# A range check on the softmax sums, a guarded second program behind a branch, and an instruction order read from a list

## The chip, the cores and the metric

The kernel runs on one core of a Trainium2 chip. A core has five instruction streams that run side by side and meet at semaphores: PE (TensorE, the matrix engine), ACT (ScalarE), DVE (VectorE), POOL (GpSimd) and SP (SyncE, which here only issues DMA transfers). The metric is the device time of one execution in microseconds. A change of under 0.2% of this kernel's time is treated as no change.

## The reference

The program is one transformer block for 2048 tokens of width 1024: an adaptive layer norm, attention with 32 query heads that share one key and one value head of width 32, and a gated feed-forward network of width 3584. Six modulation vectors come from a conditioning vector. Cut to what matters:

```python
mod = (_silu(c) @ w_mod).reshape(c.shape[0], 6, 1, -1)
sa, ca, ga, sb, cb, gb = ...
h = _layernorm(x, axis=-1) * (1 + ca) + sa
q, k, v = h @ wq, h @ wk, h @ wv            # 32 heads of 32; one k, one v
scores = jnp.einsum('bhqd,bkd->bhqk', q, k) * Dh ** (-0.5)
p = softmax(scores, axis=-1)                # the maximum of each query is subtracted
o = jnp.einsum('bhqk,bkd->bhqd', p, v)
x = x + ga * (o @ wo)
h = _layernorm(x, axis=-1) * (1 + cb) + sb
x = x + gb * ((_silu(h @ w1) * (h @ w3)) @ w2)
```

## The kernel before

The 2048 tokens are cut into 8 blocks of 256 queries (`n`), and the 32 heads into 8 groups of 4 (`f`). One pair (n, f) is a unit, so there are 64 units. A unit goes through the 2048 keys in 8 steps of 256 keys. One such step, `s_exp` (line 950), is called a score block here: 8 matmuls fill four PSUM banks with scores (tile `S<-QT,KT` in the profile), and ACT takes the exponential of them in two instructions of 128x1024 (`U<-S`). There are 512 score blocks, numbered S0 to S511 in this text in the order of PE's stream, and 1024 exponentials. The scores are not shifted: exp is taken of the scaled score as it is, and the division by the sum comes at the end.

What follows a score block: `pairs` and `fold` (lines 970, 979) add the exponentials on DVE (`PS<-U`, `PS<-PS`); `dens` (line 993) finishes the sums on PE with a matrix of ones (`PB<-PS,ONES`); `av_mm` (line 984) multiplies by the values (`PB<-U,V`, 64 matmuls for a unit); `attend` (line 1024) takes the reciprocal of the sums on DVE (`RC<-RB`), spreads it and scales the result into `QT`.

When the 8 units of a block of queries are done, its output projection (`wo`), its second layer norm, 14 pieces of the gated network (`slab`: 64 matmuls on `W`, one tanh on ACT, two products on DVE) and 4 pieces of the last matrix (`quarter`: 56 matmuls on `W2S`) follow. PE does them in between the score blocks of the next block of queries. So ACT has the exponentials all the time, and PE has, after each score block, some filling work from the block before. After S511 the last block's network is left for PE alone.

Many of the filling matmuls exist in two forms: one product of 128x128 weights, or four products of 32-row column tiles beside each other (`32x256` and `32x512` rows); the form is picked when the order is made.

The order of the work is made when the kernel is built. `build` describes each piece of work as a node of a graph with an engine (or two to choose from), a duration, a due time `vt` and the keys it reads and writes. `Placer.run` (line 294) then places the nodes one by one: `choose` (line 365) takes, for each engine, the candidate with the smallest due time among those that could start soon, and the engine that could start first gets its piece. The table `PLAN` (line 116) holds, for every 8 score blocks, the tolerances of that choice and offsets to the due times by kind of work and engine. `commit` gives a session of PE work one of the free PSUM banks (two of the eight, `PB`, until the last exponentials free the others). `emit` works out the semaphore waits. The result is one fixed list of instructions for each engine; all of them are played through `play` at line 22, so every instruction of the profile has the line L22, and the tiles tell them apart.

At the end SP waits for the transfers of the output (`finish`, L527) and all engines leave the block (L531).

The lines that the change touches, beside the table:

```python
            best = None
            for e, lst in ready.items():
                c = self.choose(e, lst)
...
    pl.run()
    pl.finish("sp", outs)
    pl.emit_all()
```

Of the kernel before, what the change touches and what calls it, by code (L numbers as in the profile page):

```python
# [8 lines left out]
P = 128  # L9
# [33 lines left out]
class Graph:  # L43
# [64 lines left out]
    def alias(self, new, old):  # L108
# [7 lines left out]
PLAN = [  # L116
    (0, 0.08, 0.11, 0, 1.1, {"an/dve": 11, "av/dve": 9, "d0/sp": -38, "d1/sp": 10, "d11/sp": 2, "d12/sp": -4,
     "d2/sp": 51, "d3/sp": -151, "d6/sp": 67, "d7/sp": 32, "d8/sp": -29, "ev/act": -21, "k/pe": -26, "k/dve": 40,
     "ln/pe": -51, "ln/act": 32, "ln/dve": -11, "ln/pool": 57, "mc/pe": 52, "mc/sp": -2, "mod/pe": -62,
     "mod/dve": 10, "nm/act": 79, "pair/dve": -129, "q/pe": 3, "q/dve": -57, "quarter/pe": 11, "quarter/dve": -2,  # L120
     "s/pe": 67, "s/act": -3, "slab/pe": -5, "slab/act": 81, "slab/dve": 30, "v/pe": -8, "wo/pe": -78, "wo/dve": 1,
     "wo/sp": 36}),
    (0, 0.36, 0.11, 1, 1, {"an/dve": 8, "av/pe": -111, "av/dve": 2, "d0/sp": -31, "d1/sp": 16, "d10/sp": -66,
     "d12/sp": 63, "d13/sp": -1, "d3/sp": -14, "d5/sp": 2, "d7/sp": 84, "d8/sp": -2, "ev/act": -29, "k/pe": -36,
     "k/dve": -9, "kb/pe": 72, "ln/dve": 124, "mod/dve": -5, "nm/act": 32, "pair/dve": -104, "quarter/dve": 2,
     "s/pe": 55, "s/act": 107, "slab/pe": -26, "slab/act": -5, "slab/dve": 33, "slab/sp": 94, "v/dve": -118,
     "v/pool": -34, "wo/pe": -76, "wo/dve": 4, "wo/pool": -59, "wo/sp": 21, "d11/sp": 0, "d2/sp": 0, "d6/sp": 0,
     "ln/pe": 0, "ln/act": 0, "ln/pool": 0, "mc/pe": 0, "mc/sp": 0, "mod/pe": 0, "q/pe": 0, "q/dve": 0,
     "quarter/pe": 0, "v/pe": 0}),
    (0, 0.14, 0.18, 2, 2.9, {"q/dve": -32, "wo/dve": -44, "slab/act": 0}),  # L130
    (0.06, 0.11, 0.27, 0, 3.9, {"av/dve": 9, "d0/sp": -58, "d1/sp": 20, "d10/sp": 257, "d13/sp": 2, "d2/sp": 3,
     "d3/sp": -2, "d4/sp": 1, "d8/sp": 83, "ev/act": -11, "k/pe": -49, "k/dve": 1, "kb/dve": -7, "ln/pe": -5,
     "mc/pe": 63, "mc/sp": 5, "nm/act": 30, "out/sp": 1, "s/act": 114, "slab/sp": 4, "v/dve": 3, "v/pool": -26,
     "wo/pe": -78, "wo/dve": 14, "wo/pool": -23, "an/dve": 0, "d12/sp": 0, "d7/sp": 0, "ln/dve": 0, "mod/dve": 0,
     "pair/dve": 0, "q/dve": 0, "quarter/dve": 0, "s/pe": 0, "slab/pe": 0, "slab/dve": 0, "wo/sp": 0, "av/pe": 0,
     "d5/sp": 0, "kb/pe": 0}),
    (0, 0.11, 0.05, 0, 0.6, {"d6/sp": 19, "ev/act": -9, "k/pe": -81, "wo/pool": 7, "s/act": 0}),
    (0, 0.11, 0.05, 0, 0.6, {}),
    (0.13, 0.12, 0.23, 0, 0.7, {"av/pe": -5, "d0/sp": -4, "d10/sp": -68, "d3/sp": -46, "d9/sp": 72, "ev/act": -16,
     "kb/pe": 2, "ln/dve": -11, "mc/pe": -7, "mod/dve": -3, "q/dve": -85, "q/sp": -6, "quarter/pe": 4,  # L140
     "slab/act": 82, "slab/dve": 33, "slab/sp": 16, "wo/pe": -5, "wo/dve": 3, "wo/pool": 15, "av/dve": 0,
     "d1/sp": 0, "d2/sp": 0, "d6/sp": 0, "k/pe": 0, "k/dve": 0, "ln/pe": 0, "mc/sp": 0, "nm/act": 0, "d13/sp": 0,
     "v/dve": 0, "v/pool": 0, "d4/sp": 0, "kb/dve": 0, "out/sp": 0}),
    (0.24, 0.09, 0.2, 1, 1.4, {"av/pe": -4, "d7/sp": 78, "ev/act": -13, "ln/pool": -2, "mod/pe": 5,
     "pair/dve": -16, "slab/act": 83, "d0/sp": 0, "mod/dve": 0}),
    (0.24, 0.09, 0.02, 1, 0.4, {"d2/sp": -4}),
    (0.07, 0.17, 0.24, 1, 0.1, {"d1/sp": 31, "d3/sp": 24, "d6/sp": 8, "d7/sp": -38, "ev/act": 20, "k/dve": 31,
     "kb/pe": 6, "ln/dve": -16, "ln/pool": 60, "mc/pe": 2, "mc/dve": 35, "nm/act": -28, "out/sp": 2,
     "pair/dve": -28, "q/dve": -49, "quarter/pe": -1, "slab/act": 10, "v/dve": 20, "wo/pool": -13, "d2/sp": 0,
     "d8/sp": 0, "mod/pe": 0, "slab/dve": 0, "wo/pe": 0, "wo/dve": 0, "d10/sp": 0, "slab/sp": 0, "d9/sp": 0,  # L150
     "q/sp": 0}),
    (0, 0.11, 0.17, 2, 2.8, {"d7/sp": -42, "k/dve": 34, "mod/dve": -56, "slab/act": -17, "q/dve": 0, "out/sp": 0}),
    (0, 0.11, 0.2, 2, 2.8, {"ev/act": 21}),
    (0, 0.11, 0.24, 1, 3.2, {"d1/sp": 8, "d3/sp": 21, "d7/sp": -38, "ev/act": 20, "k/dve": 31, "mod/dve": -60,
     "pair/dve": -30, "slab/act": 10, "v/pe": 39}),
    (0, 0.11, 0.24, 1, 3.2, {}),
    (0, 0.16, 0.15, 1, 3.2, {"d1/sp": 31, "d3/sp": 24, "kb/pe": 10, "ln/dve": -15, "mc/dve": 38, "q/dve": -16,
     "v/dve": 2, "v/pe": 0}),
    (0.06, 0.11, 0.15, 1, 0.1, {"d1/sp": 7, "ln/pool": 59, "pair/dve": -45, "v/dve": 24, "q/dve": 0}),
# [97 lines left out]
class Placer:  # L257
# [6 lines left out]
    FULL = 36.0  # L264
    FETCH = 24.0

    def __init__(self, g, banks, later, plan):
        self.g = g
        self.plan = []
        off = {}  # L270
# [1096 lines left out]
```

## Time and profile before

| what | value |
|---|---|
| time, median of 3 runs | 1136.85 us (1136.72, 1136.85 and 1138.08) |
| the profiled execution, first to last instruction | 1137.5 us; the page lists no other time of it |
| PE busy | 1102.1 us, 97% |
| DVE busy | 989.8 us, 87% |
| ACT busy | 1020.1 us, 90% |
| POOL busy | 39.1 us, 3% |
| mean granted TensorE clock | 0.992 |
| transfers | 209.64 MB, mean 184 GB/s |

The page names the instructions by tile (out<-in), since they share one line. "Idle before" and the bracket in a row of the timeline give how long the engine stood still ahead of that instruction and what it then got; "issue" there means that it waited for nothing that the profile shows. PEld is the weight load of PE, which runs beside its matmuls.

### The profile page before, as it was taken

Reading aid. Unit: us, or ns where it says so; the run is one execution under the profiler, and the core shown is the slowest. Engines: PE = TensorE matmul, PEld = TensorE weight load, DVE = VectorE, ACT = ScalarE, POOL = GpSimd, SP = SyncE. Lnnn points to the kernel's source line nnn. Section 1 sums busy time; section 2 is a strip of 40 time slices with the busy share of each in tenths; the row PEclk is TensorE's granted clock in tenths of the full one; section 3 lists DMA queues with packets and bytes.
Section 4 is the critical chain, followed back from the end, with each engine's and each line's share of the span. In section 5 each row is a group of like instructions: output and inputs, shape, how many; then the busy total and the mean of one; then the engine's idle time right before and its main releaser. Section 6 shows DMA issues by size and latency. Waiting matters only on the chain.

```text
span 1137.5 us, 37371 instructions
## 1 busy us (share of the span) xinstructions
PE 1102.1 (97%) x16835; PEld 752.4 (66%) x16860; DVE 989.8 (87%) x1617; ACT 1020.1 (90%) x1159; POOL 39.1 (3%) x91
## 2 busy tenths in 40 slices
PE   5999998999899999999999999999999999999998
PEld 4744536766467766777577766776567757776887
DVE  7998999999989989998999899998989899997442
ACT  5999999999999999999999999999989999994110
POOL 5200000000000000000000000000000000000000
PEclk9999989999999999999999999999999999999999
DMA  9320586675756666865596577868686558767993
GB/s 347 104 76 22 166 217 187 193 205 139 168 150 194 190 176 160 240 190 151 137 287 192 151 190 202 227 193 216 142 245 192 156 152 226 210 198 197 239 240 103
DMA packets 381535, 209.64 MB, mean 184 GB/s; under 512 B 17600, under 2 KB 373184, under 8 KB 381376
## 3 DMA queue, kind: packets, MB, share of 16 engines
q1 hardware_dynamic: 380944, 207.11, 65.9%
q8 instruction: 133, 2.18, 0.8%
q14 instruction: 26, 0.21, 0.1%
q10 hardware_dynamic: 432, 0.13, 0.0%
HBM read 199.89 MB, written 4.19 MB: 179 GB/s over the span
## 4 chain that ended last, share of the span: by engine, by line
PE 48%; ACT 42%; DVE 6%; DMA 1%; issue 1%; SPq 1%; POOL 0%; DVEq 0%
ACT U L22 39%; PE PB L22 34%; PE S L22 14%; ACT HT L22 3%; DVE PS L22 2%; DMA W<-in_A_wq_dram 1%; DVE ST L22 1%; SPq L22 1%; DVE X L22 1%; DVE RB L22 0%; DVE QT L22 0%; DVE HT L22 0%; DVE XNB L22 0%; DVE WO L22 0%; DVE MV L22 0%
## 5 line engine op out<-in xcount | busy, mean ns | idle before, releaser
L22 ACT ACTIVATE U<-S 128x1024 bf16<-128x1024 f32 x1024 | 966.6, 1142 | 11.5 <-PE S L22 10.7
L22 DVE TENSOR_TENSOR PS<-U 128x2048 bf16<-128x2048 bf16 x256 | 308.2, 1216 | 12.0 <-ACT U L22 10.1
L22 DVE TENSOR_TENSOR PS<-PS 128x1024 bf16<-128x1024 bf16 (+1 forms) x420 | 282.5, 689 | 2.5
L22 PE MATMUL PB<-QT,W 128*128 128x256 bf16 (+1 forms) x2688 | 228.1, 276 | 0.4 <-DVE HT L22 0.4
L22 PE MATMUL S<-QT,KT 32*128 32x256 bf16 x4096 | 204.7, 274 | 10.1 <-ACT U L22 7.8
L22 PEld LDWEIGHTS PB<-QT,W 128*128 128x128 bf16 (+1 forms) x2688 | 171.2, 98 | 42.0 <-issue 23.6
L22 PE MATMUL PB<-W2S,HT 128*128 128x256 bf16 x1512 | 189.3, 273 | 0.0
L22 PEld LDWEIGHTS PB<-W2S,HT 128*128 128x128 bf16 x1512 | 137.4, 98 | 41.5 <-issue 22.0
L22 PEld LDWEIGHTS S<-QT,KT 32*128 32x128 bf16 x4096 | 60.8, 92 | 139.5 <-ACT U L22 130.9
L22 PE MATMUL PB<-U,V 128*32 128x256 bf16 x4096 | 130.9, 276 | 3.5 <-issue 2.3
L22 PEld LDWEIGHTS PB<-U,V 128*32 128x32 bf16 x4096 | 101.8, 97 | 27.8 <-issue 15.3
L22 PE MATMUL PB<-QT,HT 128*128 128x256 bf16 (+1 forms) x1216 | 117.0, 273 | 0.0
L22 PE MATMUL PB<-HT,W 128*32 128x512 bf16 (+2 forms) x884 | 99.2, 343 | 3.1 <-DVE XNB L22 1.0
L22 PEld LDWEIGHTS PB<-QT,HT 128*128 128x128 bf16 (+1 forms) x1216 | 86.4, 97 | 21.0 <-issue 11.4
L22 ACT ACTIVATE HT<-PB 128x512 bf16<-128x512 f32 (+1 forms) x105 | 77.0, 733 | 7.9 <-PE PB L22 7.8
L22 DVE SCALAR_TENSOR_TENSOR HT<-HT,PB 128x512 bf16<-128x512 bf16 x100 | 68.3, 683 | 6.7 <-ACT HT L22 6.5
L22 PEld LDWEIGHTS PB<-HT,W 128*128 128x128 bf16 (+1 forms) x896 | 50.6, 97 | 34.3 <-issue 13.4
L22 DVE TENSOR_TENSOR HT<-HT,PB 128x512 bf16<-128x512 bf16 x100 | 68.2, 682 | 4.4 <-PE PB L22 3.1
L22 ACT ACTIVATE HT<-S 128x512 bf16<-128x512 f32 (+1 forms) x17 | 12.1, 721 | 58.9 <-PE S L22 58.9
L22 DVE STREAM_TRANSPOSE RB<-PB 128x256 f32<-128x256 f32 x63 | 28.0, 444 | 33.8 <-PE PB L22 33.4
L22 PE MATMUL PB<-WO,QT 128*128 128x512 bf16 (+1 forms) x260 | 53.2, 381 | 1.4 <-issue 0.6
L22 POOL TENSOR_SCALAR RS<-MV 128x1 f32<-128x1 f32 x32 | 10.2, 322 | 1009.3 <-DVE MV L22 1008.6
(111 smaller groups left out, 661.7 us busy)
## 6 DMA issues: line engine op xcount, KB each, us to landing
W<-in_B_w_dram SPq DMA_DIRECT2D x150, 512.0 KB, 4.6
W2S<-in_B_w_dram SPq DMA_DIRECT2D x30, 1792.0 KB, 8.5
HT<-in_B_w_dram SPq DMA_DIRECT2D x74, 512.0 KB, 4.7
W2S<-in_w_mod_dram SPq DMA_DIRECT2D x8, 1024.0 KB, 6.3
X<-in_A_x_dram SPq DMA_DIRECT2D x8, 512.0 KB, 7.2
U<-in_w_mod_dram SPq DMA_DIRECT2D x4, 1024.0 KB, 12.2
out_dram<-X SPq DMA_DIRECT2D x7, 512.0 KB, 7.7
W2S<-in_A_x_dram SPq DMA_DIRECT2D x5, 512.0 KB, 9.7
```

The costliest lines, as they stand in the source:

```text
L22: return getattr(e, call[0])(*call[1], **call[2])
```

## The change

Four things change.

1. The reciprocals of the sums are kept for a whole block of queries (`RC` grows from 8 to 2x8x8 columns), and after the 8 units of a block two small DVE instructions on 128x64 (`in_range`) multiply into a tile `FINE` whether each reciprocal lies between 1e-18 and 1e18. `FINE` is set to 1 by POOL at the start. That is 16 instructions.
2. `verdict`: after the last block one DVE reduction, one PE matmul of 1 column with the ones matrix and one DVE comparison write the tile `AGAIN`, which is 1 if any reciprocal was out of range.
3. At the end of its list every engine waits for `AGAIN`, loads it into a register, and branches: if it is not 0, a second, complete program runs, in which `shift` finds each query's maximum and three more matmuls for each head subtract it ahead of the exponential. It stands in each engine's instruction stream behind the branch. SP's wait for the output transfers, which stood behind its last transfer, now stands behind the branch.
4. The table `PLAN` is replaced for the first program by `ORDER`, a list of all 7306 nodes in the order in which they are to be placed, with a mark (`b`) where the second engine is to be taken. `choose` is still called, with the one node of the list as its candidate. The second program is still placed by the rule, with one row of `PLAN`.

The diff, cut to its core (the body of `build` is moved one level in, as `program(guarded)`, which the cut leaves out):

```diff
-PLAN = [
-    (0, 0.08, 0.11, 0, 1.1, {"an/dve": 11, "av/dve": 9, "d0/sp": -38, "d1/sp": 10, "d11/sp": 2, "d12/sp": -4,
...
+PLAN = [(0, 0.11, 0.15, 1, 2.0, {})]
+
+
+ORDER = """
+7 1 11 0 4 2 5 8 3 6 16 12 9 13 10 17 18 60 22 15 19 59 20 27 14 21 28 412 29 37 30 31 23 24 26 32 36 77 33 38 61 39
...
-            for e, lst in ready.items():
+            lists = ready
+            if self.order:
+                i, k = self.order[len(g.nodes) - left]
+                assert g.nodes[i].npred == 0
+                lists = {g.nodes[i].alts[k][0]: [g.nodes[i]]}
+            for e, lst in lists.items():
                 c = self.choose(e, lst)
...
+        def both(eng, name):
+            for fn in self.ops[name]:
+                fn(eng)
+            eng.wait_ge(sem[flag.sem], flag.val)
+            again = eng.value_load(tile)
+            with eng.If(again != 0):
+                for s, v in last.items():
+                    if v:
+                        eng.wait_ge(sem[s], v)
+                for fn in second.ops[name]:
+                    fn(eng)
+            if name == "sp":
+                for n in outs:
+                    eng.wait_ge(sem[n.sem], n.val)
...
+    LOW, HIGH = 1e-18, 1e18
...
-    RC = sb("RC", [P, 8], F32)
+    RC = sb("RC", [P, 2, NC, 8], F32)
+    FINE = sb("FINE", [P, NC, 8], BF16)
+    FINE1 = sb("FINE1", [P, 1], BF16)
+    AGAIN = sb("AGAIN", [P, 1], mybir.dt.int32)
...
+        if not guarded:
+            op("pool", lambda: [lambda e: e.memset(FINE[:], 1.0)], 0.1, writes=["FINE"], vt=-100)
...
+                    if guarded:
+                        calls += [lambda e, g=g, t=t, kk=kk: e.matmul(
+                            BANK[2 * r[g // 2] + g % 2][:, kk * B:(kk + 1) * B], ONES[:], SHIFT[:, t, g, :], start=False,
+                            stop=t == 2) for t in range(3) for g in range(4)]
...
+            rc = RC[:, n % 2, f]
+            op("dve", lambda: [lambda e: e.reciprocal(rc, RB[:, 0, :].rearrange("p (a r) -> p a r", r=32)[:, :, 0])],
+               0.12, reads=["RBD"], writes=[("RC", n % 2, f)], vt=vt)
...
+        def in_range(n):
+            G.tag = "ok"
+            k = [("RC", n % 2, f) for f in range(NC)]
+            for lim, cmp in ((LOW, ALU.is_ge), (HIGH, ALU.is_le)):
+                op("dve", lambda lim=lim, cmp=cmp: [lambda e: e.scalar_tensor_tensor(
+                    FINE[:], RC[:, n % 2], lim, FINE[:], cmp, ALU.mult)], 0.15, reads=k + ["FINE"], writes=["FINE"], vt=64.0 * n + 80)
+
+        def verdict():
+            G.tag = "ok"
+            vt = 64.0 * NB + 20
+            op("dve", lambda: [lambda e: e.tensor_reduce(FINE1[:], FINE[:].rearrange("p a b -> p (a b)"), mybir.AxisListType.X,
+                                                         ALU.min)], 0.15, reads=["FINE"], writes=["FINE1"], vt=vt)
+            s = Sess()
+            op("pe", lambda b: [lambda e: e.matmul(BANK[b][:, 0:1], ONES[:], FINE1[:], start=True, stop=True)], 0.07,
+               reads=["ONES", "FINE1"], writes=["sum"], vt=vt, mode="F", sess=s, post=0.145)
+            return op("dve", lambda b: [lambda e: e.tensor_scalar(AGAIN[:], BANK[b][:, 0:1], P - 0.5, None, ALU.is_lt)], 0.1,
+                      reads=["sum"], writes=["AGAIN"], vt=vt, sess=s)
...
+    pl, outs, flag = program()
+    second, outs2, _ = program(True, pl)
+    second.finish("sp", outs2)
+    pl.emit_all(second, flag, AGAIN[0:1, 0:1], outs)
```

How far the list departs from the order before: on PE 3694 of the 4112 common pieces of work stand in the same relative order, on DVE 1150 of 1608, on ACT 1135 of 1155, on SP 277 of 309. Counted at every 32nd score block, PE has had the same amount of filling work by then in both orders, and behind S511 the same 433 pieces are left to it, with the verdict's matmul as one more. So the list moves work by a few places.

The first place is PE from S79 to S82, where the first block of queries has gone over to its network. `PB<-U,V` is a unit's product with the values, `PB<-HT` and `PB<-HT,W` are the network's products, `PB<-PS,ONES` finishes the sums. Before:

```order
L22 MATMUL PB<-HT,W 128x256 x12
L22 MATMUL S<-QT,KT 128x256 x8
L22 MATMUL PB<-HT,W 128x256 x14
L22 MATMUL S<-QT,KT 128x256 x8
L22 MATMUL PB<-PS,ONES 32x256 x4
L22 MATMUL PB<-U,V 32x256 x64
L22 MATMUL PB<-HT 32x256 x8
L22 MATMUL S<-QT,KT 128x256 x8
L22 MATMUL PB<-HT 32x256 x48
L22 MATMUL S<-QT,KT 128x256 x8
L22 MATMUL PB<-HT 32x256 x8
L22 MATMUL PB<-HT 128x256 x10
```

After:

```order
L22 MATMUL PB<-HT,W 128x256 x20
L22 MATMUL S<-QT,KT 128x256 x8
L22 MATMUL PB<-HT,W 128x256 x6
L22 MATMUL PB<-PS,ONES 32x256 x4
L22 MATMUL S<-QT,KT 128x256 x8
L22 MATMUL PB<-HT 128x256 x12
L22 MATMUL S<-QT,KT 128x256 x8
L22 MATMUL PB<-U,V 32x256 x64
L22 MATMUL PB<-HT 128x256 x4
L22 MATMUL S<-QT,KT 128x256 x8
L22 MATMUL PB<-HT 128x256 x14
```

The run of 64 value products, which stood right behind the sums and ahead of 8 column-tile matmuls, now stands ahead of S82 instead of S81, while the sums have gone from ahead of S81 to ahead of S80, and the network's products there have all become 128-wide.

The second place is PE around S375, some six blocks of queries in. Before:

```order
L22 MATMUL PB<-QT,HT 128x256 x8
L22 MATMUL PB<-QT,W 128x256 x8
L22 MATMUL S<-QT,KT 128x256 x8
L22 MATMUL PB<-PS,ONES 32x256 x4
L22 MATMUL PB<-QT,W 32x256 x96
L22 MATMUL S<-QT,KT 128x256 x8
L22 MATMUL PB<-W2S,HT 128x256 x12
```

After:

```order
L22 MATMUL PB<-QT,HT 128x256 x10
L22 MATMUL PB<-QT,W 128x256 x8
L22 MATMUL S<-QT,KT 128x256 x8
L22 MATMUL PB<-PS,ONES 32x256 x4
L22 MATMUL PB<-QT,W 32x256 x64
L22 MATMUL S<-QT,KT 128x256 x8
L22 MATMUL PB<-QT,W 128x256 x8
L22 MATMUL PB<-W2S,HT 128x256 x4
```

The unbroken run of 4 and 96 column-tile matmuls is cut to 4 and 64; the rest comes after the next score block, in the 128-wide form.

The third place is PE around S409 to S411. Before:

```order
L22 MATMUL PB<-PS,ONES 32x256 x4
L22 MATMUL PB<-QT,W 32x256 x32
L22 MATMUL S<-QT,KT 128x256 x8
L22 MATMUL PB<-U,V 32x256 x64
L22 MATMUL PB<-QT,W 32x256 x8
L22 MATMUL S<-QT,KT 128x256 x8
L22 MATMUL PB<-QT,W 32x256 x48
L22 MATMUL S<-QT,KT 128x256 x8
L22 MATMUL PB<-QT,W 32x256 x8
```

After:

```order
L22 MATMUL PB<-PS,ONES 32x256 x4
L22 MATMUL PB<-QT,W 32x256 x40
L22 MATMUL S<-QT,KT 128x256 x8
L22 MATMUL PB<-QT,W 32x256 x56
L22 MATMUL PB<-U,V 32x256 x8
L22 MATMUL S<-QT,KT 128x256 x8
L22 MATMUL PB<-U,V 32x256 x24
L22 MATMUL PB<-QT,W 32x256 x24
L22 MATMUL PB<-U,V 32x256 x8
L22 MATMUL S<-QT,KT 128x256 x8
L22 MATMUL PB<-U,V 32x256 x24
L22 MATMUL PB<-QT,W 32x256 x8
```

The value products of the unit, which were one run of 64, are spread over three gaps and mixed with the network's column-tile matmuls.

The fourth is the end of DVE's stream. Before:

```order
L22 TENSOR_TENSOR HT<-S,GBR 128x256
L22 TENSOR_TENSOR X<-X,HT 128x256
L22 TENSOR_TENSOR HT<-S,GBR 128x256
L22 TENSOR_TENSOR X<-X,HT 128x256
L531 UNCONDITIONAL_BRANCH
```

After:

```order
L22 TENSOR_TENSOR HT<-PB,GBR 128x256
L22 TENSOR_TENSOR X<-X,HT 128x256
L22 TENSOR_TENSOR HT<-S,GBR 128x256
L22 TENSOR_TENSOR X<-X,HT 128x256
L719 TENSOR_LOAD AGAIN
L720 COMPARE_AND_BRANCH
```

DVE's last work is unchanged; what was the jump out of the block is now the load of `AGAIN` and the branch past the second program. The same pair has been put at the end of each of the other four streams.

More of the change, by code (lines that the diff above doesn't have):

```diff
@@ L265, with __init__ @@
     FETCH = 24.0
-    def __init__(self, g, banks, later, plan):
+    def __init__(self, g, banks, later, plan, first=None, order=None):
         self.g = g
@@ L292, in __init__, with read @@
         self.warm = None
+        self.order = self.read(order) if order else None
+        if first is not None:
+            self.sem, self.dma_sem = first.sem, first.dma_sem
+            self.count, self.dma_cnt = dict(first.count), dict(first.dma_cnt)
+            for e in self.ops:
+                self.known[e] = first.finals()
+    @staticmethod
+    def read(order):
+        seq = []
+        for x in order.split():
+            k = int(x[-1] == "b")
+            a, _, z = x.rstrip("b").partition("-")
+            seq += [(i, k) for i in range(int(a), int(z or a) + 1)]
+        return seq
     def run(self):
```

1617 lines of the change are left out of this document (889 added, 728 removed), and 45 rows, old and new, of tables (ORDER, PLAN).

## The prediction

> **What bounds the kernel now.** I read the page first (busy shares, chain), then the stages, then ACT's own waits.
>
> ```profile
> span 1137.5 us, 37371 instructions
> PE 1102.1 (97%) x16835; PEld 752.4 (66%) x16860; DVE 989.8 (87%) x1617; ACT 1020.1 (90%) x1159; POOL 39.1 (3%) x91
> PE 48%; ACT 42%; DVE 6%; DMA 1%; issue 1%; SPq 1%; POOL 0%; DVEq 0%
> ```
>
> PE and ACT share the chain, so the stages have to be told apart:
>
> ```profile
> core 0: us, PE busy (x) PEld busy (x) DVE busy (x) ACT busy (x) POOL busy (x), PEclk, DMA share, GB/s
> 440.00:680.00 240.00, 239.10 (x3684) 165.31 (x3681) 221.35 (x351) 238.83 (x274) 1.95 (x4) 1.00 0.72 197
> 1040.00:1137.50 97.50, 94.64 (x867) 81.24 (x860) 39.33 (x72) 8.36 (x14) 1.69 (x4) 1.00 0.78 206
> ACT U L22 <- PE S L22: 10.7, 15, 2.2
> ```
>
> In the middle ACT works 238.83 of 240 us on exponentials and the tanh, so it sets the pace, and PE is just in time for it: over the whole run ACT stands ahead of an exponential for only 10.7 us, 15 times. DVE has 18.65 us free of 240. In the last 97.5 us the exponentials are over and PE alone is the bound (94.64 busy; the rest is the end, where the last DVE work and the last transfer follow). So an order of PE's work can win at most those 10.7 us ahead of the last exponential, and nothing behind it, since the same 433 pieces remain there. Whatever is put behind the last transfer or beside it can only lengthen the end.
>
> **The moved work, place by place.** ACT's larger waits by place:
>
> ```profile
> 149.09 7.51 ACT L22 ACTIVATE U<-S 128x1024 bf16<-128x1024 f32 x8 [0.67 <-PE S L22]
> 157.33 14.83 ACT L22 ACTIVATE U<-S 128x1024 bf16<-128x1024 f32 x16 [0.73 <-PE S L22]
> 172.67 6.59 ACT L22 ACTIVATE U<-S 128x1024 bf16<-128x1024 f32 x7 [0.51 <-PE S L22]
> 187.40 1.93 PE L22 MATMUL PB<-U,V 128*32 128x256 bf16 x64 [0.59 <-DVE HT L22]
> 189.94 2.86 ACT L22 ACTIVATE U<-S 128x1024 bf16<-128x1024 f32 x3 [1.19 <-PE S L22]
> 391.81 48.80 ACT L22 ACTIVATE U<-S 128x1024 bf16<-128x1024 f32 x53 [0.47 <-PE S L22]
> 763.77 2.79 PE L22 MATMUL PB<-QT,W 128*32 128x256 bf16 x96
> 766.94 3.77 ACT L22 ACTIVATE U<-S 128x1024 bf16<-128x1024 f32 x4 [0.47 <-PE S L22]
> 834.55 0.29 PE L22 MATMUL PB<-U,V 128*32 128x256 bf16 x4 [2.33 <-issue]
> 835.46 1.94 ACT L22 ACTIVATE U<-S 128x1024 bf16<-128x1024 f32 x2 [2.18 <-PE S L22]
> 838.49 1.94 ACT L22 ACTIVATE U<-S 128x1024 bf16<-128x1024 f32 x2 [1.09 <-PE S L22]
> 840.59 1.02 ACT L22 ACTIVATE U<-S 128x1024 bf16<-128x1024 f32 x1 [0.16 <-PE S L22]
> ```
>
> S375 (766.94): a run of 96 matmuls took 2.79 us and ACT then waited 0.47. In the list a third of the run goes to the next gap; two thirds take 1.9, which is 0.9 shorter than the run that cost 0.47. Term: -0.47; at worst 0. The same run stands unchanged at other block edges (391.81 is one), so their 0.47 stays.
>
> S81 (189.94): PE waited 0.59 for DVE, which had yet to free the bank, did 64 value products in 1.93 and 8 more matmuls; ACT waited 1.19. In the list these products come one score block later, ahead of S82, when DVE is through, and with 4 network matmuls behind them: a gap below the 2.79 that costs 0.47, with no wait in front. Ends: -1.19 if nothing is left, 0 if the wait moves along to S82. I take -0.9, near the first, because the longest run in the trace leaves under half as much.
>
> S61 to S73 (149 to 173): three waits, 1.91 together. The modulation chunk's matmuls go one gap earlier and one output-projection piece is evened out. DVE is what PE waits for there, and its amount of work stays. Ends: -1.9 and +1; I take -0.3, nearest to no change.
>
> S410 (834.55): PE stopped for 2.33 us inside one run of 64 matmuls, waiting for nothing that the profile shows, and ACT lost 2.18 + 1.09 + 0.16 = 3.43. What surrounds it:
>
> ```profile
> DMA  9999999999999999999999999999999999999999
> q8 instruction: 1, 0.02, 0.9%
> q8 instruction: 133, 2.18, 0.8%
> ```
>
> The first two lines are for 828 to 836 us: every slice has the transfer engines full, and one 16 KB packet of instructions came in. The third is the whole run: 133 such packets, one in 8.6 us on average (1137.5/133). Around S410 column-tile matmuls of 29 ns each (2.79/96), with a weight load each, eat instructions faster than elsewhere. So I read the stop as instructions that came late; that is an inference. The list mixes the 64 value products with other column tiles (156 of them in the three gaps up to S411 become 164), which keeps that stretch as dense. I take it as staying: 0. If it goes, -3.43; that is the first rival.
>
> Head: the scaled first columns of `wq` go from six on DVE and two on POOL to five and three.
>
> ```profile
> 24.28 2.03 POOL L22 TENSOR_SCALAR WO<-W,MODC 128x256 bf16<-128x256 bf16 x2 [1.68 <-DMA W<-in_A_wq_dram]
> 27.11 0.14 DVE L22 COPY QBI<-PB 128x2 f32<-128x2 f32 x1
> 27.30 0.77 PEld L22 LDWEIGHTS PB<-HT,WO 128*128 128x128 bf16 x8 [0.97 <-DVE QBI L22]
> ```
>
> PE started the first query projection at 27.30, on DVE's copy. Three tiles on POOL end at 24.28 + 3 x 1.02 = 27.34, so +0.1 at most. SP's early transfers are only exchanged among themselves ahead of the same one of `wq`. ACT has two evacuations instead of two norms after the first exponential, about as long. Term: 0.
>
> **The added work.**
>
> ```profile
> L22 DVE RECIPROCAL RC<-RB 128x8 f32<-128x8 f32 x64 | 12.9, 201 | 1.8
> L22 DVE COPY VBR<-PB 128x32 f32<-128x32 f32 x1 | 0.2, 182 | 0.0
> L22 DVE TENSOR_TENSOR V<-PB,VBR 128x128 bf16<-128x128 f32 x4 | 1.2, 288 | 0.1
> 160.00:170.00 10.00, 9.84 (x91) 3.77 (x92) 9.83 (x17) 10.00 (x12) 0.79 (x2) 1.00 1.14 287
> ```
>
> A check on 128x64 lies between 182 and 288 ns; I take 0.22. Sixteen of them, the reduction and the comparison make 18 x 0.22 = 4.0 us of DVE. In a block of 125 us there are 2 of them, 0.44, against some 9.7 us free (18.65 x 125/240): hidden. In the first block they come after S67, between the waits at 157 and 173, where DVE is full (9.83 of 10 in the last row); there up to 0.44 reaches ACT. Term: +0.2 (0 to +0.44). What waits behind them is an evacuation or a pair sum. The verdict's matmul lies in the last stage, where PE is the bound: one column, behind a reduction that comes right after the last `QT`; other products stand between. Term +0.1 (0 to 0.5). The comparison is long done when the flag is read. POOL's memset runs while POOL waits for the first data: 0.
>
> **The end.** All engines now load `AGAIN` and branch. PE and ACT do so while DVE still works; DVE and SP are last.
>
> ```profile
> 1125.21 10.64 SPq L22 DMA_DIRECT2D out_dram<-X  x4
> 1135.19 0.29 DVE L22 TENSOR_TENSOR X<-X,HT 128x256 bf16<-128x256 bf16 x1
> SPq L527 <- DMA out_dram<-X: 0.9, 1, 0.9
> SPq L531 <- PEq L531: 0.2, 1, 0.2
> SCC<-in_c_dram ACTq DMA_DIRECT2D x1, 2.0 KB, 2.4
> 0.72 0.10 POOL L22 MEMSET NH<- 128x1 f32 x1 [0.29 <-POOLq L1352]
> ```
>
> SP issued its last transfer by 1135.85 and then waited 0.9 for it. Load and branch go into this 0.9, and what is longer is added. The trace has no register load: below it is bounded by a message between sequencers (0.2), above by the smallest transfer from issue to landing (2.4). I take 0.9, a third of the way, since it is one word and needs no descriptors. The branch jumps over a whole program: below, the start's barrier and jump took 0.29; above, 2.33, the stop at 834.55 if that was a late instruction packet. I take 1.6, nearer to the upper, since the target lies behind some hundred transfers on SP and thousands of instructions on DVE. Sum 0.9 + 1.6 - 0.9 = +1.6; from 0 (0.2 + 0.29 is hidden) to 2.4 + 2.33 - 0.9 = +3.8.
>
> The Trainium skill speaks against this change here: "Runtime: NRT & Kernel Launch", Instruction fetch mechanics, says that a taken branch whose target is outside the two-page window must wait until that page is fetched, and "DMA: Bandwidth & Descriptors", Latency and other measured facts, gives a register load some 0.6 us at least. Before's trace has no such branch to confirm it. With 0.6 for the load and 2.33 for the fetch the end would be an estimated +2.0.
>
> **Sum.** -0.47 - 0.9 - 0.3 + 0.2 + 0.1 + 1.6 = +0.2. Against the profiled execution's 1137.5 that is 1137.7; the median of the three runs, 1136.85, stands 0.65 lower, so I forecast 1137.1. A difference of 0.2%, 2.3 us, is about what a measurement of this kernel can tell from no change.
>
> **Rivals.**
>
> Faster: the stop at S410 does not come back, because packets and transfers meet differently. For it: it came once in 512 gaps, and the list takes apart the very run in which it came. Against it: the stretch stays as dense and the transfers as full. Time: 1137.1 - 3.4 = 1133.7.
>
> Slower by the end: load and jump at their upper ends, +3.8 instead of +1.6: 1139.3. For it: two things on SP one after the other with only 0.9 of cover. Against it: the transfer queues are idle then. It decides from an end of 3.7 on (2.3 + 1.4 of the other terms).
>
> Slower by the order: the list makes new long gaps ahead of S79, S82, S238 and S383 (20 products, or 64 column tiles and 4 products). If each costs 0.47 as the 2.79 run does, S81 and S61 to S73 win nothing and the checks cost 0.44: 1136.85 - 0.47 + 1.9 + 0.44 + 0.1 + 1.6 = 1140.4. Against it: the order before has such gaps too, and ACT waits only 15 times in all.
>
> The change does not do what it says: a reciprocal counts as out of range and the second program runs, at least 1137 more, some 2300 us. Against it: sums over 2048 keys of small scores are far from 1e18.
>
> **Chances.** Forecast 0.45 (own range 1135.3 to 1139.0: S81 and S61 to S73 at their gains, or the end near 3.5), stop gone 0.25, end at its upper bound 0.15, order with new waits 0.13, second program 0.02. Faster by over 0.2% (below 1134.6): most of the stop's case, 0.20, and 0.04 of the forecast's: 0.24. Slower (above 1139.1): 0.11 of the end's case, 0.11 of the order's, 0.02, and 0.06 of the forecast's: 0.30. Within 0.2%: 0.46. The range reaches from the stop's case to the order's: 1133.3 to 1140.4.
>
> **What would show it.** The changed profile should have no wait of ACT at S375 and under 0.5 at S81 to S82; 0.47 still at the other block edges; a stop of PE on "issue" near S410 of about 2 us; DVE checks of about 0.22 us; the last DVE work as long before the end as now plus 1.6, with SP on a load and a jump. I am wrong if ACT's waits ahead of exponentials sum to over 14 us or under 6, or if the end after DVE's last work grows by over 3.

## The result, and the profile after

The changed kernel takes 1139.8 us (median of 20 runs, 1137.88 to 1141.51); the kernel before, in 20 runs beside it, 1137.71. The ratio is 1.0018, 95% interval 1.0012 to 1.0025: some 2.1 us slower, a bit under the 0.2% bound, which lies inside the interval. The second program did not run.

The page of the changed kernel, the lines that answer to those of before (the first is the span, the second busy time by engine, the third the chain that ended last, the others the queues that bring instructions):

```profile
span 1138.1 us, 37341 instructions
PE 1102.5 (97%) x16818; PEld 753.6 (66%) x16845; DVE 993.6 (87%) x1634; ACT 1020.1 (90%) x1159; POOL 42.8 (4%) x93
PE 47%; ACT 44%; DVE 3%; DMA 2%; issue 1%; SPq 1%; POOL 1%; DVEq 0%
q8 instruction: 134, 2.20, 0.8%
q14 instruction: 33, 0.27, 0.1%
```

Bounds and chain are as before. One thing has to be read rightly first: a span is not the time of the execution. In every run here, of all the kernels, the time lies 1.7 to 2.1 us above the span (the changed kernel's profiled execution took 1140.01 us at a span of 1138.1; the kernel before has 1137.9 at 1136.0 in one run, 1135.55 at 1133.6 in another). So the profile of before that the prediction was made from, span 1137.5, belongs to an execution of some 1139.4 us, 1.7 above that kernel's median: it shows one of its slow executions.

**ACT's waits** by place, of the changed kernel, and their sum over the run (last line: total, times, longest):

```profile
152.87 3.77 ACT L22 ACTIVATE U<-S 128x1024 bf16<-128x1024 f32 x4 [0.96 <-PE S L22]
157.94 12.98 ACT L22 ACTIVATE U<-S 128x1024 bf16<-128x1024 f32 x14 [1.31 <-PE S L22]
171.49 7.58 ACT L22 ACTIVATE U<-S 128x1024 bf16<-128x1024 f32 x8 [0.56 <-PE S L22]
391.51 54.42 ACT L22 ACTIVATE U<-S 128x1024 bf16<-128x1024 f32 x59 [0.50 <-PE S L22]
782.11 38.99 ACT L22 ACTIVATE U<-S 128x1024 bf16<-128x1024 f32 x42 [0.55 <-PE S L22]
835.65 2.86 ACT L22 ACTIVATE U<-S 128x1024 bf16<-128x1024 f32 x3 [0.25 <-PE S L22]
961.26 2.85 ACT L22 ACTIVATE U<-S 128x1024 bf16<-128x1024 f32 x3 [0.42 <-PE S L22]
ACT U L22 <- PE S L22: 7.5, 14, 1.3
```

The waits at S81 (1.19 before) and S375 (0.47 at 766.94) are gone, and of the 3.43 at S410 0.25 is left. In their place stand 0.55 at 782.11 (S383), 0.42 at 961.26 (S476), and 2.83 instead of 1.91 between 149 and 173. Three PE rows belong to this:

```profile
151.25 1.01 PE L22 MATMUL PB<-SCC,W2S 128*128 128x1 bf16 x32 [1.65 <-DMA W2S<-in_w_mod_dram]
834.75 0.29 PE L22 MATMUL PB<-QT,W 128*32 128x256 bf16 x4 [0.34 <-issue]
1069.67 0.39 PE L22 MATMUL S<-QT,W 128*128 128x256 bf16 x2 [0.75 <-DVE HT L22]
```

The modulation chunk's matmuls, one gap earlier in the list, wait 1.65 us for their own weights; the 2.33 us stop is down to 0.34; and the last stage has a new wait for DVE.

**The end.** First the last DVE work of the changed kernel, then, in the order of time, the flag's loads on DVE and SP, their branches, and what each does next (L730 and L728); the last line is the kernel before, SP's waits behind its last transfer. Columns of the lower rows: count, shortest/median/longest in ns, first and last start:

```profile
1133.43 0.29 DVE L22 TENSOR_TENSOR X<-X,HT 128x256 bf16<-128x256 bf16 x1
```

```profile
L719 DVEq TENSOR_LOAD <-AGAIN x1: 545/545/545, 1133.5 to 1133.5; - x1
L719 SPq TENSOR_LOAD <-AGAIN x1: 502/502/502, 1134.2 to 1134.2; - x1
```

```profile
L720 DVEq COMPARE_BRANCH  x1: 72/72/72, 1134.0 to 1134.0; - x1
L720 SPq COMPARE_BRANCH  x1: 53/53/53, 1134.7 to 1134.7; - x1
```

```profile
L730 DVEq DRAIN  x1: 57/57/57, 1137.0 to 1137.0; - x1
```

```profile
L728 SPq EVENT_SEMAPHORE  x6: 17/28/28, 1137.3 to 1137.7; - x6
```

```profile
L527 SPq EVENT_SEMAPHORE  x6: 17/28/28, 1135.9 to 1137.1; - x6
```

The load is 0.50 us; the branch itself is short, but then nothing happens on SP for 2.58 us (1134.75 to 1137.33) and on DVE for 2.9. In that hole the trace has this, from 1134.9 to 1136.2, where the program's own transfers move next to nothing:

```profile
q8 instruction: 1, 0.02, 6.3%
q14 instruction: 2, 0.02, 3.9%
```

By the transfer records the two packets of 8 KB on q14 land at 1135.52 and 1135.98. The records do not name the engine that a packet is for. If the first is DVE's, which branched first, and the second SP's, DVE goes on (1136.99) 1.47 us behind its own, and SP (1137.33) 1.35. From DVE's last work to the end it is 4.41 us, against 2.06 before: +2.35.

**Where the time went**, by ACT's 1024 exponentials. Each column is the lateness that a stretch added against the profile of before (negative: it won). The e2 column is the old order with everything else of the change, the next four have the list; e1, e3 and e4 are told below:

| stretch of exponentials | e2 (old order) | changed kernel | e1 | e3 | e4 |
|---|---|---|---|---|---|
| up to the first exponential | +0.14 | +0.30 | +0.26 | +0.33 | +0.56 |
| 0 to 116 | 0.00 | -0.45 | -0.49 | -0.45 | +0.58 |
| 116 to 154 (S58 to S77) | +0.14 | +1.18 | +0.02 | +2.09 | +0.58 |
| 154 to 158 (S79) | +0.01 | +0.29 | +0.29 | +0.29 | +0.28 |
| 158 to 170 (S81) | -0.01 | -0.87 | -0.86 | -0.87 | -0.87 |
| 170 to 304 (S139, S145, S151) | +0.09 | -0.92 | -0.92 | -0.88 | -0.91 |
| 304 to 748 (S274 to S280 above all) | +0.05 | +0.70 | +0.65 | +0.65 | +0.65 |
| 748 to 768 (S375, S383) | 0.00 | +0.16 | +0.16 | +0.16 | +0.16 |
| 768 to 816 | 0.00 | -0.07 | -0.07 | -0.07 | -0.07 |
| 816 to 830 (S410) | -0.37 | -3.57 | -3.82 | -3.57 | -3.43 |
| 830 to 1000 (S476) | 0.00 | +0.61 | +0.55 | +0.74 | +0.79 |
| 1000 to the last exponential | +0.24 | -0.07 | -0.08 | -0.07 | -0.08 |
| behind it, to the end of DVE's last work | +0.02 | +0.95 | +0.69 | +0.81 | +0.63 |
| all of it | +0.31 | -1.75 | -3.62 | -0.83 | -1.14 |

The same list gives nearly the same numbers in four executions (to 0.05 us in most rows, to 0.4 at S410 and behind it), except ahead of S77. There PE's clock comes in: the records have it at half speed for stretches of 3.4 us. Two of them lie between 146 and 160 us in the profile of before, where they bring the mean clock of each 10 us (the column behind POOL's) down to 0.83:

```profile
140.00:150.00 10.00, 9.88 (x191) 4.41 (x180) 9.07 (x17) 9.33 (x11) 0.00 (x0) 0.83 0.53 176
150.00:160.00 10.00, 8.56 (x157) 3.98 (x159) 8.55 (x19) 9.27 (x11) 0.00 (x0) 0.83 0.77 199
```

The changed kernel and e2 have two there as well, e1 one, e3 three, and e4 two and one more near 36 us, to which its +0.58 in the row before fits. Without the row of S410 the four profiles with the list are 0.2 (e1) to 2.7 us (e3) later than the profile of before, and e2 is 0.7 later: outside S410 no gain of the list is shown (e1, ahead of e2, has one half-clock stretch less).

### The profile page after: what moved, and what is told of

It is laid out like the page before. It is cut to its first block, busy times and chain, and to the rows that moved or that the text cites. A ratio compares the mean times of both kernels' runs of the same rounds, so it can differ in the third digit from the quotient of the medians.

```text
span 1138.1 us, 37341 instructions
## 1 busy us (share of the span) xinstructions
PE 1102.5 (97%) x16818; PEld 753.6 (66%) x16845; DVE 993.6 (87%) x1634; ACT 1020.1 (90%) x1159; POOL 42.8 (4%) x93
## 4 chain that ended last, share of the span: by engine, by line
PE 47%; ACT 44%; DVE 3%; DMA 2%; issue 1%; SPq 1%; POOL 1%; DVEq 0%
ACT U L22 42%; PE PB L22 34%; PE S L22 14%; ACT HT L22 3%; DVE PS L22 1%; DMA W<-in_A_wq_dram 1%; SPq L22 1%; DVE HT L22 1%; DMA W2S<-in_w_mod_dram 1%; POOL RS L22 0%; DVE ST L22 0%; DVE QT L22 0%; POOL WO L22 0%; DVE X L22 0%; DVE RB L22 0%
## 5 line engine op out<-in xcount | busy, mean ns | idle before, releaser
L22 PE MATMUL PB<-QT,W 128*128 128x256 bf16 (+1 forms) x2632 | 223.7, 273 | 0.5 <-issue 0.3
L22 PEld LDWEIGHTS PB<-QT,W 128*128 128x128 bf16 (+1 forms) x2632 | 167.4, 97 | 41.4 <-issue 23.0
L22 PE MATMUL PB<-QT,HT 128*128 128x256 bf16 (+1 forms) x1288 | 123.9, 273 | 0.5 <-issue 0.5
L22 ACT ACTIVATE HT<-PB 128x512 bf16<-128x512 f32 (+1 forms) x110 | 81.3, 739 | 31.0 <-PE PB L22 30.9
L22 PEld LDWEIGHTS PB<-QT,HT 128*128 128x128 bf16 (+1 forms) x1288 | 91.0, 97 | 22.6 <-issue 11.9
L22 POOL TENSOR_SCALAR RS<-MV 128x1 f32<-128x1 f32 x32 | 13.3, 417 | 1003.2 <-DVE MV L22 997.0
L22 ACT ACTIVATE HT<-S 128x512 bf16<-128x512 f32 (+1 forms) x13 | 9.4, 728 | 36.9 <-PE S L22 36.9
```

The costliest lines, as they stand in the source:

```text
L22: return getattr(e, call[0])(*call[1], **call[2])
```

## The experiments

**Order against end: four kernels side by side.** e1 leaves the guard out:

```diff
-            eng.wait_ge(sem[flag.sem], flag.val)
-            again = eng.value_load(tile)
-            with eng.If(again != 0):
...
-    second, outs2, _ = program(True, pl)
-    second.finish("sp", outs2)
-    pl.emit_all(second, flag, AGAIN[0:1, 0:1], outs)
+    pl.emit_all(None, flag, AGAIN[0:1, 0:1], outs)
```

> The new order, the checks and the verdict stay; load, branch and second program are left out. Theory (the order gains, the end pays): the order gains the 1.76 us by which DVE's last work came earlier in the changed kernel's profile (1133.43 against 1135.19), and the 2.0 us from that work to the end are as before: some 1.8 us below the kernel before, device time about 0.6 us above its span. Rival (the order is worth nothing, the gain in that one profile was chance): within 0.5 us of the kernel before.

Measured: 1137.35, ratio to the kernel before 0.9998 (0.9988 to 1.0008); 2.07 us from DVE's last work to the end. So the rival holds: the list (with its checks) is worth nothing that these runs can tell, between 1.4 us won and 0.9 lost by the interval, and the changed kernel's 2.1 us are the end. The 0.6 us expected between time and span, and the 1.3 that e2 to e4 expect outside the span, were a misreading (above).

e2 keeps all but the list, which now holds the old order with the twenty added pieces:

> The list holds the order of the kernel before, with the twenty added pieces put in; checks, load, branch and second program stay. Theory: the order's 1.8 us are lost and the end's price stays whole: 4.4 us from DVE's last work to the end instead of 2.0 and 1.3 more outside the span, so 3.6 us above the kernel before; the 2.33 us stop at S410 comes back if it belongs to the order. Rival (the order is worth nothing): as the changed kernel, 2.1 above the kernel before.

Measured: 1141.15, ratio 1.0029 (1.0016 to 1.0042), 3.3 us above: nearer to the theory's 3.6 than to the rival's 2.1, but the interval (1.8 to 4.8) holds both, so it does not contradict e1. ACT at S410, and SP's next instruction behind the jump:

```profile
835.50 1.94 ACT L22 ACTIVATE U<-S 128x1024 bf16<-128x1024 f32 x2 [1.81 <-PE S L22]
838.10 1.94 ACT L22 ACTIVATE U<-S 128x1024 bf16<-128x1024 f32 x2 [0.65 <-PE S L22]
```

```profile
L725 SPq EVENT_SEMAPHORE  x6: 17/28/28, 1139.6 to 1139.9; - x6
```

The stop is back with the old order, and the end is 4.62 us. Exponential 1000 comes only 0.05 us later than in the profile of before, which has as many half-clock stretches at the same places; but 0.37 of that was won by a shorter stop, and 0.14 was lost ahead of the first exponential, where no check stands. The other rows up to exponential 1000 add 0.28 us, and the rows up to the last one 0.52: that is the most that the sixteen checks can have cost here, and rows of up to 0.2 us also come and go between two profiles of the kernel before.

e3 keeps load and branch, but behind the branch stand only the waits:

```diff
                     if v:
                         eng.wait_ge(sem[s], v)
-                for fn in second.ops[name]:
-                    fn(eng)
```

> All as in the changed kernel, but behind the branch stand only the waits: the second program is left out, the flag is still loaded and the branch still taken. Theory (the distance of the jump costs): SP's 2.58 us from the branch to its next instruction shrink to about the 0.4 that POOL needed over its short second program, the load's 0.5 is hidden behind the last transfer (1.2 us from the end of its issue to landing), and the 1.3 outside the span go: as the kernel without guard, 1.6 to 1.8 below the kernel before. Rival (load and branch cost, wherever they lead): the end stays 4.4 us long and the time 2.1 above the kernel before.

Measured: 1137.7, ratio 0.9998 (0.9989 to 1.0007). SP's branch, and the waits behind it:

```profile
L720 SPq COMPARE_BRANCH  x1: 58/58/58, 1135.6 to 1135.6; - x1
```

```profile
L726 SPq EVENT_SEMAPHORE  x6: 17/28/28, 1136.1 to 1136.5; - x6
```

0.45 us from the branch to the next instruction instead of 2.58; the end is 2.27 us, 0.2 above before. The price is the distance of the jump, not load or branch. In the changed kernel the jumps show it too: POOL, over some 120 instructions, needed 0.41 us; SP over some 350 and DVE over some 4300 needed 2.58 and 2.9. The Trainium skill says this in "Runtime: NRT & Kernel Launch", Instruction fetch mechanics: a taken branch to a place outside the window of instructions at hand has to wait for a fetch. The traces agree: 2.58 us against 0.45.

e4 branches earlier on SP and DVE, ahead of their last six pieces, which stand in both arms; all of the guard is kept:

```diff
+            ops = self.ops[name]
+            cut = len(ops) - {"sp": 6, "dve": 6}.get(name, 0)
+            for fn in ops[:cut]:
...
             with eng.If(again != 0):
+                for fn in ops[cut:]:
+                    fn(eng)
...
+            with eng.Else():
+                for fn in ops[cut:]:
+                    fn(eng)
```

> Nothing is left out. SP and DVE load the flag and branch ahead of their last six pieces of the first program, which stand once in each arm; the arm taken lies behind the second program. Theory (the jump costs where nothing hides it): SP jumps near 1107 us, with nothing to do, and DVE inside a wait of 4.96 us, so the end is as short as before, the instructions behind the end are there by then, and the time is that of the kernel without guard: 1.6 to 1.8 below the kernel before. Rival (the mere second program costs the 1.3 outside the span): 0.3 to 0.5 below. Rival (the jump costs anywhere): 2.1 above.

Measured: 1137.76, ratio 0.9999 (0.9990 to 1.0007), with the branches at

```profile
L722 SPq COMPARE_BRANCH  x1: 53/53/53, 1108.4 to 1108.4; - x1
L722 DVEq COMPARE_BRANCH  x1: 72/72/72, 1122.7 to 1122.7; - x1
```

and an end of 2.08 us. The time is that of e1, by the ratios; neither lies the expected 1.6 to 1.8 us below the kernel before, since the list gained nothing. The jump itself did not get shorter: SP's next instruction, the first of its last six pieces, came at 1114.54, 6.1 us behind its branch, where the changed kernel had it at 1107.95; nothing waited for it. DVE's jump lay inside its wait of 4.96 us for PE. So the guard cost no measurable time (the interval goes from 1.1 us won to 0.8 lost) where nothing waited for what the engine did next.

**What is the stop at S410, and is it always there?** e5 is the old order with the list's S404 to S414 put in, and the early branch. PE there, as the kernel has it (o: old order, +: put in):

```
 o  PB<-PS,ONES x4, PB<-QT,W 32x256 x32 | S | PB<-U,V x64, PB<-QT,W 32x256 x8 | S | PB<-QT,W 32x256 x48 | S
 +  PB<-PS,ONES x4, PB<-QT,W 32x256 x40 | S | PB<-QT,W 32x256 x56, PB<-U,V x8 | S | PB<-U,V x24, PB<-QT,W 32x256 x24, PB<-U,V x8 | S
```

> Nothing is left out: the order of the kernel before with the list's S404 to S414 put in, checks, and the branch ahead of the last six pieces of SP and DVE as in the kernel with the early branch. Theory (the stop at S410 belongs to the old order, comes in the larger half of its runs and costs 3.4 us where it comes; the runs of the kernel before lie around 1135.6 and around 1138.7): no stop, and a median near the lower group, 1135.6 to 1136.3, some 1.8 below that of the kernel before. Rival (the list gains by all its moves together, S410 being one chance among them): within 0.5 of the kernel before.

Measured: 1135.22 (1134.65 to 1136.98), ratio 0.9979 (0.9968 to 0.9990), 2.1 below the kernel before: as the theory has it. ACT runs through the place without a wait:

```profile
830.19 7.56 ACT L22 ACTIVATE U<-S 128x1024 bf16<-128x1024 f32 x8
```

By the median this is the fastest of all these kernels and does all that the changed one does: some 4.4 us below it by the two ratios (1.0018 and 0.9979).

The kernel before, three more profiles. The first two took 1139.26 and 1138.98 us, the third 1136.22:

> The kernel before, unchanged, for its profile. Theory: if the time is near 1138.7 there is the stop at S410 of some 2 us and a stretch of half clock right behind it; if it is near 1135.6 there is neither. Rival: the stop is there in both cases, and the clock alone makes the difference.

> The kernel before, unchanged, a second profile: the same two cases, and with luck the one that the first did not show.

> The kernel before, unchanged, a further profile. In the three that there are it took 1139 us and stopped 1.7 to 2.3 us at S410. Theory: if this one takes under 1137 us, PE does not stop there for over 0.5 us, and the packet near 832 us comes less than 360 PE instructions after the one before it. Rival: under 1137 us with the stop as long as ever.

PE at the place, in the second and the third:

```profile
834.00 0.29 PE L22 MATMUL PB<-U,V 128*32 128x256 bf16 x4 [2.24 <-issue]
```

```profile
832.81 0.29 PE L22 MATMUL PB<-U,V 128*32 128x256 bf16 x4 [0.65 <-issue]
```

And the third run's instruction packet of PE (q8): it came between 829.9 and 831.4 us, in the profile of before between 831.5 and 833.2:

```profile
q8 instruction: 1, 0.02, 4.9%
```

The same program, 3 us apart, with a long stop and a short one. (0.65 us is a little over the 0.5 set down for the third run, 365 instructions a little over the 360.) From the transfer records of all these traces, the packet next to S410: its start after exponential 816 began, the PE instructions begun between the start of the packet before and its own, when it landed, when PE went on, how far behind the landing, and the stop (e6 is told below):

| trace | start, us | instructions | landed | PE goes on | behind it | stop |
|---|---|---|---|---|---|---|
| before | 3.06 | 493 | 833.07 | 834.55 | 1.48 | 2.33 |
| b2 | 2.96 | 477 | 832.52 | 834.00 | 1.48 | 2.24 |
| e2 | 2.86 | 453 | 833.33 | 834.59 | 1.26 | 1.96 |
| b1 | 2.51 | 457 | 834.40 | 835.77 | 1.37 | 1.69 |
| e6 | 3.39 | 413 | 832.47 | 833.79 | 1.32 | 1.08 |
| b3 | 1.31 | 365 | 831.27 | 832.81 | 1.54 | 0.65 |
| changed kernel | 2.96 | 291 | 833.33 | 834.75 | 1.42 | 0.34 |
| e5 | 0.41 | 354 | 830.31 | - | - | none |

PE goes on 1.3 to 1.5 us after the landing whatever the stop is, and in the traces of the old order the stop grows with the packet's lateness. This fits a late instruction packet, as the prediction inferred; e7 below tests it. The half clock behind it is not always there (b1 has none): it is a second price, the waits of 1.09 and 0.16 us behind the stop in the profile of before. "Runtime: NRT & Kernel Launch" of the Trainium skill (Instruction fetch mechanics) counts the crossing of a block of instructions as mostly hidden; here it cost up to 2.33 us, and the measurement decides.

e6 adds to e5 two more stretches of the list in which the table shows gains, S77 to S89 and S133 to S152:

> As the run before it in this call, with the list's S77 to S89 and S133 to S152 put in as well, the places where ACT's exponentials in the changed kernel's profile gained on those of before (0.9 us at S81, 0.55 and 0.2 near S145 and S151), while S61 to S73, S238, S274 to S280, S383, S476 and the last stage, where they lost, keep the old order. Theory: 1.3 to 1.6 below the run before it, so 3.0 to 3.5 below the kernel before. Rival (waits only move along to the next full gap): no more than 0.5 below the run before it.

Measured: 1136.54, ratio 0.9990 (0.9979 to 1.0001), 1.3 above e5. In its trace both gains are there: 0.88 us between exponentials 160 and 170, 0.92 between 170 and 304. But the stop is back:

```profile
833.79 0.82 PE L22 MATMUL PB<-QT,W 128*32 128x256 bf16 x21 [1.08 <-issue]
```

That profile is of an execution of 1135.83 us, 0.7 below e6's median, and its DVE ends only 0.13 us later than in the profile of e5; that other executions of e6 stop longer, which would make up the 1.3, is not shown. The stretches changed the number of instructions ahead of S410 (128-wide products in place of column tiles): PE's records have 25494 ahead of exponential 816, against 25591 in e5 (the count differs by up to 23 between profiles of one program), and so the packets cut elsewhere. e7 tests that: the kernel before, with 100 instructions more at PE's start:

```diff
+                for _ in range(200):
+                    e.wait_ge(self.sem["pool"], 1)
                 for fn in self.ops["pe"]:
                     fn(e)
```

> The kernel before with one addition: PE, which stands idle until 9.1 us, first waits 200 times for a count that is long reached, which adds 100 instructions to its stream and moves no piece. Theory (the stop at S410 is an instruction packet that is asked for too late, so it hangs on where the 16 KB packets cut PE's stream; in five profiles the stop grew with the number of PE instructions between two packets there: 354 none, 347 then 291 0.34 us, 413 1.1, 457 1.7, 493 2.3): the packet near 832 us comes some 100 instructions earlier, the stop is under 0.5 us, ACT loses under 0.7 there instead of 1.5 to 3.4, and the median lies 1 to 2.5 below the kernel before. Rival (the stop comes from the full transfer queues or the narrow column tiles in that place): the stop stays at 1.5 us or more and the time within 0.5 of the kernel before.

Measured: 1138.64, ratio 1.0006 (0.9993 to 1.0018). The stop is gone but for 0.20 us, no piece of work being moved; PE's only row on "issue" there, and its first work:

```profile
836.48 1.60 PE L22 MATMUL PB<-QT,W 128*32 128x256 bf16 x17 [0.20 <-issue]
```

```profile
11.74 1.05 PE L22 MATMUL PB<-U 128*32 128x256 bf16 x16 [11.74 <-DVE ST L22]
```

Its packets there start at 826.37 and 833.36 us, with 302 and 293 instructions since the ones before, where the profile of before has a single one, at 831.89 with 493. From exponential 816 to 830 it won 3.55 us against the profile of before. The time did not follow, since the waits took PE until 11.64 us, and the first exponential came 2.08 us later: I had taken PE's 9 us of idleness as enough. That would leave this profile's execution (1137.76) 1.7 us below the one of before; the median of e7 lies 0.9 above its profile and its times spread from 1136.83 to 1140.50, so whether the stop is gone in its other executions is not shown. e8 is e6 with the same waits:

> The old order with three stretches of the list and the early branch, with the same 200 waits at PE's start. Theory: the 1.1 us that ACT lost at S410 in its profile go with the packet's place, what S81 and S145 to S151 won stays: 1 to 1.4 below the run without the waits, 2 to 2.8 below the kernel before. Rival: the stop stays, 0.6 to 1.2 below the kernel before as without the waits.

Measured: 1136.46, ratio 0.9990 (0.9978 to 1.0002). With 25594 instructions ahead of exponential 816, about as many as e5, its trace has no stop, as e5's has none, and its packet starts 0.15 us behind that exponential. But it is 1.28 us later than e6 at the first exponential: gain and price cancel, and its number was missed for that reason.

e9 goes back to the list and undoes S57 to S76:

> The list with the early branch, and S57 to S76 put back to the old order, all engines and transfers: the modulation chunk's matmuls are again behind the value projections, so none waits for its transfer (0.7 to 1.65 us in the list's profiles). Theory: the 0.8 to 1.4 us that the list lost between S58 and S79 against the old order come back: some 1.0 below the kernel with the early branch, so 0.8 to 1.4 below the kernel before. Rival (that loss is only the half clock, which falls there in either order): within 0.4 of the kernel with the early branch.

Measured: 1136.58, ratio 0.9992 (0.9981 to 1.0004), below e4 by 0.8 us by the ratios (1.2 by the medians, which were not taken side by side). The wait for the modulation weights is gone from the trace, and at two half-clock stretches, as in e4 and the changed kernel, exponentials 116 to 154 lose 0.26 us instead of 0.58 and 1.18. Much of that is lost again right behind, at S79 (0.80 instead of 0.28): from the first exponential to exponential 170 it is 0.36 ahead of the changed kernel. The direction is the theory's; the intervals are too wide to exclude the rival.

## Why the prediction was right, point by point

Beside the kernel before, +0.2 us was said and +2.1 measured: "within 0.2%" holds, just. The 1139.8 themselves lie above the forecast's own range (1139.0) and inside the whole one (1140.4); 0.86 us of the distance to 1137.1 is the base, 1136.85 in three runs and 1137.71 in twenty. So the statement holds partly by luck: on the median both halves missed upwards, the order's by 1.2 us and the end's by 0.7, and their sum stays just under the bound. In the profile misses of opposite sign hid each other: 3.6 us won at S410 against 1.8 lost elsewhere.

- **The end, +1.6.** Mis-sized: +2.35 in the trace. Load 0.50 (0.9 taken), jump 2.58 (1.6 taken, 2.33 the upper bound, which is exceeded). The shape held: load and jump on SP, one after the other, partly under the last transfer. The estimate of +2.0 with the Trainium skill's load of 0.6 ("DMA: Bandwidth & Descriptors", Latency and other measured facts) was nearer; the load is 0.46 to 0.55 here.
- **S410, 0.** Wrong for the profiled case. The premise that the stretch "stays as dense" was true, and the reading of the stop as a late packet fits all the traces. The step that failed is "I take it as staying": a packet's place depends on all the instructions ahead of it, and the list moved that. The faster rival's mechanism came true (-3.57), not its time: the prediction took the stop of its one profile for that of every execution, and set that profile's span beside the median time (1137.5 and 1136.85). The kernel before takes 1135.1 us at its fastest and 1137.7 on the median, and e5 gains some 2.1 by taking the stop away; so on the median the stop was worth nearer 2 than 3.4.
- **S81, -0.9.** -0.87, in four traces.
- **S375, -0.47.** The wait went as said, 0.68 us there, but came back at S383 with 0.73, one of the four new gaps that the slower rival named. S79, another, cost 0.29; S82 is within S81's sum, and S238 cost nothing.
- **S61 to S73, -0.3.** Wrong sign in its own row: +0.4 to +1.0 with as many half-clock stretches (the changed kernel and e4 against e2). The cause that the trace shows was not in the working: a matmul moved ahead of the arrival of its own weights, 1.65 us. Ahead of it, up to exponential 116, the list had won 0.45 us in three of four profiles, which was not in the working either; the two rows together are between 0 (e1 against b3, one stretch each there) and +0.6 (the changed kernel against e2, two each).
- **Not in the sum:** 0.7 us between S152 and S374, 0.6 at S476, 0.6 to 0.9 behind the last exponential (0.63 to 0.95, less the 0.02 of the old order); and gains of 0.9 between S85 and S152. The statement that the order can win "nothing behind" the last exponential was right; that it could lose there was not considered.
- **Checks +0.2, verdict +0.1, head 0.** The checks take 213 ns each; e2 puts their price at 0.3 to 0.5 at most (above), against 0 to 0.44 forecast, and the verdict's at 0.02 (lateness +0.29 at the last exponential, +0.31 at the last DVE work). The first exponential came 0.30 us later, against 0.14 to 0.67 in six other traces with the old head: nothing.

The check's row, and the verdict's:

```profile
L22 DVE SCALAR_TENSOR_TENSOR FINE<-RC,FINE 128x64 bf16<-128x64 f32 x16 | 3.4, 213 | 0.2
L22 PE MATMUL S<-FINE,ONES 128*128 128x1 bf16 x1 | 0.2, 167 | 0.0
```

So the order's terms, -1.4 with checks and verdict, were really about -0.2 (e1, from -1.4 to +0.9), and the end +2.3 instead of +1.6. Beside b3, whose stop was short, three of the four profiles with the list would have looked like a loss of 1.5 us and more up to DVE's last work, and e1 like a gain of 0.4.

What stays open: why the packet near S410 is asked for or served earlier in some executions of the same program than in others, how much of e9's gain over e4 is clock, and what makes executions with the same mean clock differ by up to 2.3 us (e7 at 0.995: 1136.83 to 1139.08).

## What to carry to other kernels

A guarded second program cost nothing measurable here while the first one worked; its price was the far jump, and that can be moved to where nothing waits for the engine, by branching early and writing the last pieces into both arms. Before a stop on "issue" is put down to an order, look at more than one profile: among narrow tiles on PE the place of the instruction packets decided here, and an edit ahead of it shifts them. A gain of an order has to be checked at the next full gap, and a moved matmul against the arrival of its weights.

## What the hardware showed that was not expected

- A jump over some 350 instructions or more at the end left SP and DVE without work for 2.6 to 3.1 us (4.2 on ACT, 1107.11 to 1111.32, where nothing waited for it), over some 120 or fewer for 0.1 to 0.45. On SP it took 6.1 to 6.2 us where it came 0.7 us behind ACT's (e4, e5, e9). PE's branch is itself recorded with 3.5 to 3.8 us where it jumps far, 1131.38 to 1134.91 in the changed kernel, and 0.4 in e3.
- From the landing of an instruction packet to the next instruction it is 1.3 to 1.5 us on PE, DVE and SP, and 1.1 on ACT (landed 1110.18, next 1111.32).
- PE's clock goes to half speed for stretches of 3.4 us or multiples in a run on one core, two to four such stretches in a profile, mostly near 36, 150 and 310 us. In e5 the spread goes with them: nine runs of e5 at a mean clock of 0.995 took 1134.65 to 1135.67 us, three at 0.992 to 0.994 took 1136.29 to 1136.98. "TensorE: Matmul & The Clock Gate" of the Trainium skill (Part 1) gives a free-running window of 3413 ns, to which the stretches fit; by its table the half clock follows an idle window, while here it followed stops of 2.33, 2.24 and 1.96 us. Ahead of the stretch at 146 us, in the profile of before, PE did not stand still for over 0.3 us at a time in 8 us. What sets off the half clock in this kernel is not shown.
- 200 waits for a count long reached, which stand as 100 instructions in the trace of e7, took PE's sequencer 10.8 us (0.86 to 11.64), 0.11 us an instruction.
